# State-exchange attention with an MLP: state reads turned once through DRAM, scores of later batches kept in place, last rows in fewer transfers

## The chip, the cores and the metric

The kernel runs on one core of a Trainium2 chip. The metric is the device time in microseconds (us) of one execution; the median of several runs counts. One execution is also profiled, and the profile gives the start and the duration of each instruction on each engine: PE (matrix multiply; PEld is its weight load), ACT (activations and copies), DVE (elementwise work, reductions, 32x32 transposes), POOL, and SP, which here only issues DMAs. ACT issues DMAs too, on a queue of its own.

## The reference

For each of 8 batches and 8 heads there are 512 tokens `x` and 32 states, both of width 64. Tokens read from states, states read from tokens, and the two results, 544 rows per batch, go through one MLP of width 512 -> 2048 -> 512:

```
scores  = x @ state.T / 8        # 512 x 32
xread   = softmax(scores)  @ state
scores2 = state @ x.T / 8        # 32 x 512
sread   = softmax(scores2) @ x   # 32 x 64 per head
rows    = concat(xread, sread)   # heads side by side: (8 * 544) x 512
h       = rows @ w_in
g       = h if h >= 1, 0 if h <= -1, else (h + 1)**2 / 4
out     = g @ w_out
```

## The kernel before

Matmuls that need full precision are done as three matmuls of rounded pieces: each operand is split into a high part (names ending in `h`) and the rest (`l`), and high x high, high x rest and rest x high are added up in PSUM. So most lines of the matmul stream come in threes: L479, L480, L481 for the first MLP product (into the PSUM banks `h`), L537, L538, L539 for the second (into the accumulators `acc`).

The token rows of a batch never go through `w_in` as such. `xread` is attention times `state`, so the kernel multiplies `state` by `w_in` first (`sw_pair`, L426: eight column chunks per batch, two at a time, small matmuls of 64 rows x 32 columns of the array) and then the attention weights by that product (`g1`). `g2` is the product with `w_out`. A batch has 8 steps `(b, j)`, j = 0 to 7; step `(b, j)` issues `g1(b, j)` and then, in two parts, `g2` of the step before. Between them, the attention of the next batch b+1 is worked off:

- j = 0: `read2` (L358) of batch b, the matmuls of the state reads with the exponentials of `scores2`, already turned; `scale2`, which divides them by the sums on DVE; then the `sw` pieces 1 to 4 of batch b; then `scores` (L235) of batch b+1, 8 small products of 64 x 32 tiles into the PSUM tile with the tag `mm`, of which there is one; then `second`: the softmax over tokens, and `trade`.
- `trade` writes the exponentials `e2` to DRAM and reads them back in another order of partitions (one write and four reads, all on SP); a DVE transpose of 32x32 blocks (`turn_traded`, L336) at j = 2 completes the turn.
- j = 1: `keep2` turns the scaled state reads `rs` (128 x 128) by a PE transpose (L374, against `ident`) into another use of the tag `mm`, and `keep` copies the result on ACT (L379) into `srT`, which collects the state rows of all batches with features on the partitions.
- j = 2: `first`, the softmax over states. j = 4: the `sw` pieces 5 to 7 and piece 0 of the next batch, the last pair of them in the tag `mm`.

Batch 0 has an order of its own, written out by hand (`ORDER`, `Plan.emit`), which ends with step (0, 7); its `read2` and `keep2` are done together with those of batch 1 in steps (1, 0) and (1, 1). After it, order on each engine is set by a list scheduler: it takes instructions in program order, but an instruction whose inputs are ready may be put ahead of earlier ones while the engine would be idle by the scheduler's own reckoning. That order is fixed before the program runs; each engine then goes through its instructions strictly in turn.

After batch 7, "batch" 8 is the 256 state rows: `srT` is split by two DVE instructions (L808, L809), goes through `w_in` and `w_out` in 4 double steps, and the two blocks of 128 result rows are copied out of PSUM (L552 on ACT, L550 on DVE) and written by `store` (L559), 32 rows of one batch per transfer.

Of the kernel before, what the change touches and what calls it, by code (L numbers as in the profile page):

```python
# [8 lines left out]
F32 = mybir.dt.float32  # L9
# [4 lines left out]
ALU = mybir.AluOpType  # L14
# [94 lines left out]
def state_exchange_moe(  # L109
# [17 lines left out]
    nc = tc.nc  # L127
    B, P, NT, H, D = x.shape
    S = NT * P
    NS = 32  # L130
    DM = H * D
    NPR = H // 2
# [5 lines left out]
    TOK = S + NS  # L138
# [3 lines left out]
    small = ctx.enter_context(tc.tile_pool(name="small", bufs=1))  # L142
    const = ctx.enter_context(tc.tile_pool(name="const", bufs=1))
    work = ctx.enter_context(tc.tile_pool(name="work", bufs=2))
# [4 lines left out]
    dram = ctx.enter_context(tc.tile_pool(name="dram", bufs=2, space=bass.MemoryType.DRAM))  # L149

    def ps_acc(name):
        return ps.tile([P, DM], F32, tag="acc", bufs=4, name=name)
# [10 lines left out]
    def ps_mm(name):  # L163
        return ps.tile([P, 2, 512], F32, tag="mm", bufs=1, name=name)

    ident = small.tile([P, P], F32, name="ident")
# [14 lines left out]
    nc.gpsimd.memset(pad, 0.0)  # L181

    sb = const.tile([P, B, NPR, NS], F32, name="sb")
    srT = const.tile([P, NPR, B, NS], F32, name="srT")
    w32 = [const.tile([P, NPR, CI], F32, name=f"w32_{c}") for c in range(NC)]
    wo = {}
# [6 lines left out]
    def load_xt(b):  # L193
        xt = work.tile([P, 2, NPR, S // 2], F32, tag="xt", bufs=1, name=f"xt{b}")
        for i in range(2):
            nc.sync.dma_start(out=xt[:, i], in_=xt_in[b, i])
        return xt

    def load_xn(b):
        if b:  # L200
            xn = work.tile([P, NT, H, D], F32, tag="xn", bufs=1, name=f"xn{b}")
        else:
            xn = rawp.tile([P, NT, H, D], F32, tag="raw", name=f"xn{b}")
        nc.sync.dma_start(out=xn, in_=x[b])
        return xn

    class Attention:

# [8 lines left out]
        def scores(self, half=None):  # L217
            b = self.b
            if half != 1:
                if b:  # L220
                    sc = ps_mm(f"sc{b}")
                    self.sc = [sc[:, hh] for hh in range(2)]
                else:
                    self.sc = [ps_acc(f"sc{b}_{hh}") for hh in range(2)]
                self.z = work.tile([P, 2, S], F32, tag="z", bufs=1, name=f"z{b}")
                self.m1 = small.tile([P, 2 * NM], F32, tag="m1", name=f"m1_{b}")
                self.s1 = small.tile([P, 2 * NM], F32, tag="s1", name=f"s1_{b}")
            for pr in range(NPR):
                for hh in range(2):
                    rows = slice(hh * 64, hh * 64 + 64)  # L230
                    o = self.sc[hh][pr * NS:(pr + 1) * NS]
                    m = self.xt[rows, :, pr]
                    if half is not None:
                        o, m = o[:, half * S // 2:(half + 1) * S // 2], m[:, half]
                    nc.tensor.matmul(o, lhsT=sb[rows, b, pr], rhs=m, start=True, stop=True)  # L235

        def tokens(self, half):
            return slice(None) if half is None else slice(half * S // 2, (half + 1) * S // 2)
# [78 lines left out]
            )  # L317

        def trade(self):
            self.e2x = work.tile([P, NPR, 2 * P], F32, tag="tmp", name=f"e2x{self.b}")  # L320
            there = dram.tile([P, NT, 2 * P], F32, tag="e2d", name=f"e2d{self.b}")
            if self.b:
                nc.sync.dma_start(out=there, in_=self.e2.rearrange("p t q k -> p t (q k)"))
            else:
                for q in range(2):
                    nc.sync.dma_start(
                        out=there[:, :, q * P:(q + 1) * P], in_=self.e2[:, q].rearrange("p (t k) -> p t k", k=P)
                    )
            for t in range(NT):
                nc.sync.dma_start(  # L330
                    out=self.e2x[t * NS:(t + 1) * NS], in_=there[:, t].rearrange("(r n) k -> n r k", n=NS)
                )

        def turn_traded(self):
            e2 = self.e2.rearrange("p t q k -> p (t q k)" if self.b else "p q s -> p (q s)")
# [25 lines left out]
                        )  # L361

        def scale2(self):
            b = self.b
            self.rs = small.tile([P, 2, D], F32, tag="rs" if b else "rs_0", name=f"rs{b}")
            nc.vector.tensor_tensor(
                out=self.rs, in0=self.sr, in1=self.r2[:, :, None].broadcast_to([P, 2, D]), op=ALU.mult
            )

        def keep2(self):  # L370
            b = self.b
            self.turned2 = ps_mm(f"rt{b}") if b else atts[1].turned2
            self.rt = self.turned2[:, 0 if b else 1, :P]
            nc.tensor.transpose(  # L374
                out=self.rt, in_=self.rs.rearrange("p a d -> p (a d)"), identity=ident
            )

        def keep(self):
            nc.scalar.copy(  # L379
                out=srT[:, :, self.b], in_=self.rt.rearrange("p (g n) -> p g n", n=NS)  # L380
            )

        def second(self):
# [124 lines left out]
    def g1(b, j):  # L508
        hid = Hidden(b, j)
        for i in range(2):  # L510
            hid.product(i)
            hid.relu(i)
        hid.square()
        for i in range(2):
            hid.bound(i)
        hid.high()
        hid.low()
# [27 lines left out]
    def store(b, t):  # L545
        if t == 0:
            outs[b] = rawp.tile([P, NT, DM], F32, tag="raw", name=f"o{b}")
        o = outs[b][:, t]
        if b == B and t % 2:
            nc.vector.tensor_copy(o, acc[b][t])  # L550
        else:
            nc.scalar.copy(out=o, in_=acc[b][t])  # L552
        if b < B:
            r0 = b * TOK + t * P
            nc.scalar.dma_start(out=out[r0:r0 + P, :], in_=o)
        else:
            for i in range(4):
                r0 = (4 * t + i) * TOK + S
                (nc.sync if i % 2 else nc.scalar).dma_start(  # L559
                    out=out[r0:r0 + NS, :], in_=o[i * NS:(i + 1) * NS]  # L560
                )


# [51 lines left out]
    op = plan.op  # L615
# [25 lines left out]
    atts = {}  # L641
# [162 lines left out]
    for i, (b, j) in enumerate(steps):  # L804
        if (b, j) == (B, 0):
            sh, sl = (work.tile([P, NPR, B * NS], F32R, tag=t, name=f"s{t}") for t in ("ath", "atl"))
            src = srT.rearrange("p a b n -> p a (b n)")
            nc.vector.tensor_copy(sh, src)  # L808
            nc.vector.tensor_tensor(out=sl, in0=src, in1=sh.bitcast(F32), op=ALU.subtract)  # L809
            att_of[B] = (sh, sl)  # L810
        g1(b, j)
        if i + 1 < len(steps) and steps[i + 1][0] == B:
            for c in (2 * steps[i + 1][1], 2 * steps[i + 1][1] + 1):
                wi_split(c)
        before = steps[i - 1] if i else (0, NJ - 1)
        if b == B:
            g2(*before)
            continue
        nxt = atts[b + 1] = Attention(b + 1) if b + 1 < B and j == 0 else atts.get(b + 1)
        cut = 8 if j == 0 else 5  # L820
        g2(*before, (0, cut))
        if j == 0:
            if nxt:
                for k in (1, 0) if b == 1 else (b,):
                    atts[k].read2()
                for k in (1, 0) if b == 1 else (b,):
                    atts[k].scale2()
            halves = [
                sw_pair([(b, c), (b, c + 1)], [ps_acc(f"sw{b}_{c}_{hh}") for hh in range(2)]) for c in (1, 3)
            ]  # L830
            if nxt:
                nxt.scores()
                if b + 2 < B:
                    loaded["xt", b + 2] = load_xt(b + 2)
                loaded["xn", b + 1] = load_xn(b + 1)
            else:
                atts[b].read2()
            for split in halves:
                split()
            if nxt:  # L840
                nxt.second()
            else:
                atts[b].scale2()
        elif j == 1:
            for k in (1, 0) if b == 1 else (b,):
                atts[k].keep2()
            for k in (1, 0) if b == 1 else (b,):
                atts[k].keep()
        elif j == 2 and nxt:
            nxt.first()  # L850
        elif j == 4:
            last = [(b, 7)] + ([(b + 1, 0)] if nxt else [])
            own = ps_h(f"sw{b}_5")
            split = sw_pair([(b, 5), (b, 6)], own[1:])
            both = ps_mm(f"sw{b}_7")
            split2 = sw_pair(last, [both[:, hh] for hh in range(2)], both)
            split()
            split2()
            if nxt:
                nxt.halves()  # L860
        g2(*before, (cut, 8))
# [44 lines left out]
```

## Time and profile before

| | |
|---|---|
| time, median of 3 runs | 647.26 us (646.82 to 647.54) |
| the profiled execution's own time | 647.03 us |
| span of the profile | 645.3 us |
| PE busy | 635.3 us, 98% of the span |
| PE weight loads busy | 513.1 us, 80% |
| DVE busy | 347.0 us, 54% |
| ACT busy | 355.2 us, 55% |
| moved by DMA | 52.04 MB |

A time in the profile counts from the start of the span. A row of the timeline has the start, the duration, the engine, the line of the kernel, the operation, what it writes and reads, and in brackets how long its engine had been idle before it and what ended that. Rows that end in x2 or more join neighbours of one kind. Matmuls overlap: the distance between two starts tells what one costs, not its duration.

### The profile page before, as it was taken

How to read it: one execution, taken by the hardware profiler on the slowest of the kernel's cores; microseconds unless marked ns; L12 is line 12 of the kernel's file. 1: busy time of each engine (PE TensorE's matmuls, PEld its weight loads, DVE VectorE, ACT ScalarE, POOL GpSimd, SP SyncE). 2: the span in 40 equal slices, each digit the busy share in tenths (PEclk: the TensorE clock that was granted, in tenths of full speed). 3: DMA queues.
4: the chain of work that ended last, by engine and by line, in shares of the span. 5: the costliest groups of instructions: out<-in, count | busy, mean ns of one | idle time of the engine just before them, and what ended most of it. 6: DMA issues, size and time to landing. Idle time of an engine off the chain costs nothing.

```text
span 645.3 us, 10268 instructions
## 1 busy us (share of the span) xinstructions
PE 635.3 (98%) x4372; PEld 513.1 (80%) x4372; DVE 347.0 (54%) x492; ACT 355.2 (55%) x468; POOL 0.8 (0%) x7
## 2 busy tenths in 40 slices
PE   7899999999999999999999999999999999999997
PEld 6677777878787887878787887878787877788896
DVE  5999978642594338543574339433673344334431
ACT  4999865454565456444664457444654454444632
POOL 0000000000000000000000000000000000000000
PEclk9999999999999999999999999999999999999999
DMA  8996525000420006000520015000410010000101
GB/s 346 366 369 232 172 72 215 25 2 1 171 91 1 0 34 229 2 2 0 196 67 1 0 59 204 2 1 0 159 38 1 1 66 1 2 0 1 66 1 33
DMA packets 17757, 52.04 MB, mean 81 GB/s; under 512 B 1968, under 2 KB 7216, under 8 KB 14640
## 3 DMA queue, kind: packets, MB, share of 16 engines
q1 hardware_dynamic: 12768, 42.67, 17.9%
q10 hardware_dynamic: 4944, 8.72, 3.8%
q8 instruction: 34, 0.56, 0.4%
q14 instruction: 11, 0.09, 0.0%
HBM read 38.27 MB, written 13.11 MB: 80 GB/s over the span
## 4 chain that ended last, share of the span: by engine, by line
PE 95%; DVE 2%; ACT 1%; issue 0%; DMA 0%; ACTq 0%; POOL 0%; SPq 0%; POOLq 0%
PE acc L537 19%; PE acc L539 19%; PE acc L538 19%; PE h L479 10%; PE h L480 10%; PE h L481 10%; PE sw L426 4%; PE sc L235 1%; PE sr L358 1%; PE warmed L177 1%; DMA out_dram<-o 0%; ACT raw_o L591 0%; DVE z L274 0%; DVE sw_1l L442 0%; DVE m L253 0%
## 5 line engine op out<-in xcount | busy, mean ns | idle before, releaser
L537 PE MATMUL acc<-wo,gh 128*128 128x512 f32 x544 | 213.5, 392 | 0.0
L538 PE MATMUL acc<-wo,gh 128*128 128x512 f32 x544 | 211.9, 389 | 0.0
L539 PE MATMUL acc<-wo,gl 128*128 128x512 f32 x544 | 211.8, 389 | 0.0
L488 ACT ACTIVATE u<-h,half 128x512 f32<-128x512 f32 (+1 forms) x128 | 91.7, 716 | 179.3 <-PE h L481 170.4
L495 DVE SCALAR_TENSOR_TENSOR u<-u,h 128x512 f32<-128x512 f32 (+1 forms) x128 | 86.4, 714 | 184.2 <-ACT u L491 184.1
L537 PEld LDWEIGHTS acc<-wo,gh 128*128 128x128 f32 x544 | 102.1, 188 | 24.9 <-issue 3.7
L539 PEld LDWEIGHTS acc<-wo,gl 128*128 128x128 f32 x544 | 102.1, 188 | 21.6
L538 PEld LDWEIGHTS acc<-wo,gh 128*128 128x128 f32 x544 | 102.1, 188 | 20.6
L506 DVE TENSOR_TENSOR gl<-u,gh 128x1024 fp32r<-128x1024 f32 x68 | 83.3, 1224 | 55.3 <-ACT gh L501 55.3
L501 ACT CAST gh<-u 128x1024 fp32r<-128x1024 f32 x68 | 71.4, 1050 | 63.4 <-DVE u L495 63.4
L491 ACT ACTIVATE u<-u 128x1024 f32<-128x1024 f32 x68 | 72.2, 1061 | 1.8
L426 PE MATMUL sw<-w,sb 64*32 64x256 f32 x1024 | 32.3, 380 | 3.2 <-DVE w L599 2.2
L426 PEld LDWEIGHTS sw<-w,sb 64*32 64x32 f32 x1024 | 18.2, 106 | 12.8 <-DVE u L495 2.5
L552 ACT COPY o<-acc 128x512 f32<-128x512 f32 x33 | 19.0, 583 | 12.1 <-PE acc L539 12.1
L479 PE MATMUL h<-ath,sw_3h 128*128 128x512 f32 x64 | 25.1, 393 | 0.0
L479 PE MATMUL h<-ath,sw_5h 128*128 128x512 f32 x64 | 24.9, 390 | 0.0
L480 PE MATMUL h<-ath,sw_5l 128*128 128x512 f32 x64 | 24.9, 390 | 0.0
L481 PE MATMUL h<-atl,sw_3h 128*128 128x512 f32 x64 | 24.9, 389 | 0.0
L480 PE MATMUL h<-ath,sw_3l 128*128 128x512 f32 x64 | 24.9, 389 | 0.0
L481 PE MATMUL h<-atl,sw_5h 128*128 128x512 f32 x64 | 24.9, 389 | 0.0
L479 PE MATMUL h<-ath,sw_1h 128*128 128x512 f32 x60 | 24.4, 407 | 0.5 <-DVE u L495 0.4
L479 PE MATMUL h<-ath,sw_7h 128*128 128x512 f32 x60 | 23.5, 391 | 0.0
(160 smaller groups left out, 707.1 us busy)
## 6 DMA issues: line engine op xcount, KB each, us to landing
xt<-in_xt_dram SPq DMA_DIRECT2D x16, 512.0 KB, 5.4
raw_i<-in_moe_w_in_dram SPq DMA_DIRECT2D x8, 1024.0 KB, 7.1
raw_o<-in_moe_w_out_dram SPq DMA_DIRECT2D x8, 1024.0 KB, 11.6
xn<-in_x_dram SPq DMA_DIRECT2D x8, 1024.0 KB, 5.5
out_dram<-o ACTq DMA_DIRECT2D x32, 256.0 KB, 2.0
e2x<-e2d SPq DMA_DIRECT2D x32, 128.0 KB, 2.9
e2d<-e SPq DMA_DIRECT2D x7, 512.0 KB, 2.6
e2d<-e SPq DMA_DIRECT2D x2, 256.0 KB, 4.8
```

The source lines that it names most:

```text
L426: nc.tensor.matmul(banks[hh][pr * NS:(pr + 1) * NS, cols], lhsT=sb[rows, b, pr], rhs=w32[c][rows, pr], start=True, stop=True,)
L479: nc.tensor.matmul(o, lhsT=wh[:, k, sl], rhs=ah[:, k], start=first, stop=False)
L480: nc.tensor.matmul(o, lhsT=wl[:, k, sl], rhs=ah[:, k], start=False, stop=False)
L481: nc.tensor.matmul(o, lhsT=wh[:, k, sl], rhs=al[:, k], start=False, stop=last)
L488: nc.scalar.activation(out=u, in_=h, func=AF.Relu, scale=0.5, bias=half)
L491: nc.scalar.activation(out=self.u, in_=self.u, func=AF.Square)
L495: nc.vector.scalar_tensor_tensor(out=u, in0=u, scalar=1.0, in1=h, op0=ALU.min, op1=ALU.max)
L501: nc.scalar.copy(out=gh, in_=self.u)
L506: nc.vector.tensor_tensor(out=gl, in0=self.u, in1=gh.bitcast(F32), op=ALU.subtract)
L537: nc.tensor.matmul(a, lhsT=lh, rhs=oh, start=f == 0, stop=False)
L538: nc.tensor.matmul(a, lhsT=lh, rhs=ol, start=False, stop=False)
L539: nc.tensor.matmul(a, lhsT=ll, rhs=oh, start=False, stop=f == NF - 1)
```

## The change

Three edits.

First, the `scores` matmuls of batches 2 to 7 are tied to their place: each one gets an order edge (no wait for completion) behind the PE instruction written just before it, so the scheduler can't put it ahead of that one.

Second, the PE transposes and their ACT copies go (`keep2`, `keep`). `scale2` writes its result directly into `sread`, an SBUF tile that collects the scaled state reads of all batches. In step (7, 1) one trade through DRAM is issued for all of it, by the same function that e2 uses, and at (7, 6) in program order one DVE transpose writes `srT`. The function `trade` becomes free-standing, and for e2 it does what it did.

Third, the last rows of two batches are written by one transfer: each block of 128 rows takes two transfers of 64 rows, one from each of the two queues, in place of four of 32 rows, two from each.

```diff
+    sread = const.tile([P, NT, B, NS], F32, name="sread")
     srT = const.tile([P, NPR, B, NS], F32, name="srT")
...
+    def trade(a, name):
+
+        there = dram.tile([P, NT, 2 * P], F32, tag="there", name=f"{name}_there")
+        if a.shape[1] == NT:
+            nc.sync.dma_start(out=there, in_=a)
+        else:
+            for q in range(2):
+                nc.sync.dma_start(
+                    out=there[:, :, q * P:(q + 1) * P], in_=a[:, q].rearrange("p (t k) -> p t k", k=P)
+                )
+        traded = work.tile([P, NPR, 2 * P], F32, tag="tmp", name=f"{name}_x")
+        for t in range(NT):
+            nc.sync.dma_start(
+                out=traded[t * NS:(t + 1) * NS], in_=there[:, t].rearrange("(r n) k -> n r k", n=NS)
+            )
+        return traded
...
-                    nc.tensor.matmul(o, lhsT=sb[rows, b, pr], rhs=m, start=True, stop=True)
+                    made = nc.tensor.matmul(o, lhsT=sb[rows, b, pr], rhs=m, start=True, stop=True)
+                    if b > 1:
+                        tc.keep_in_program_order(made)
...
         def trade(self):
-            self.e2x = work.tile([P, NPR, 2 * P], F32, tag="tmp", name=f"e2x{self.b}")
...
+            self.e2x = trade(self.e2.rearrange("p t q k -> p t (q k)") if self.b else self.e2, f"e2_{self.b}")
...
         def scale2(self):
-            b = self.b
-            self.rs = small.tile([P, 2, D], F32, tag="rs" if b else "rs_0", name=f"rs{b}")
             nc.vector.tensor_tensor(
-                out=self.rs, in0=self.sr, in1=self.r2[:, :, None].broadcast_to([P, 2, D]), op=ALU.mult
-            )
-
-        def keep2(self):
-            b = self.b
-            self.turned2 = ps_mm(f"rt{b}") if b else atts[1].turned2
-            self.rt = self.turned2[:, 0 if b else 1, :P]
-            nc.tensor.transpose(
-                out=self.rt, in_=self.rs.rearrange("p a d -> p (a d)"), identity=ident
-            )
-
-        def keep(self):
-            nc.scalar.copy(
-                out=srT[:, :, self.b], in_=self.rt.rearrange("p (g n) -> p g n", n=NS)
+                out=sread.rearrange("p (q a) b d -> p q a b d", q=2)[:, :, :, self.b],
+                in0=self.sr.rearrange("p q (a d) -> p q a d", d=NS),
+                in1=self.r2[:, :, None, None].broadcast_to([P, 2, D // NS, NS]), op=ALU.mult,
             )
...
-            for i in range(4):
-                r0 = (4 * t + i) * TOK + S
+            rows = out.rearrange("(b r) d -> b r d", r=TOK)
+            for i in range(2):
+                b0 = 4 * t + 2 * i
                 (nc.sync if i % 2 else nc.scalar).dma_start(
-                    out=out[r0:r0 + NS, :], in_=o[i * NS:(i + 1) * NS]
+                    out=rows[b0:b0 + 2, S:], in_=o[i * 2 * NS:(i + 1) * 2 * NS]
                 )
...
         elif j == 1:
-            for k in (1, 0) if b == 1 else (b,):
-                atts[k].keep2()
-            for k in (1, 0) if b == 1 else (b,):
-                atts[k].keep()
+            if not nxt:
+                sreadx = trade(sread.rearrange("p t b n -> p t (b n)"), "sread")
         elif j == 2 and nxt:
             nxt.first()
+        elif j == 6 and not nxt:
+            nc.vector.transpose(
+                out=srT.rearrange("p r b n -> p (r b n)"), in_=sreadx.rearrange("p r k -> p (r k)")
+            )
```

More of the change, by code (lines that the diff above doesn't have):

```diff
@@ L319, in trade @@
         def trade(self):
-            self.e2x = work.tile([P, NPR, 2 * P], F32, tag="tmp", name=f"e2x{self.b}")
[L321 to L327, printed above, removed]
-                    )
-            for t in range(NT):
-                nc.sync.dma_start(
-                    out=self.e2x[t * NS:(t + 1) * NS], in_=there[:, t].rearrange("(r n) k -> n r k", n=NS)
-                )
+            self.e2x = trade(self.e2.rearrange("p t q k -> p t (q k)") if self.b else self.e2, f"e2_{self.b}")
         def turn_traded(self):
@@ L363, in scale2 @@
         def scale2(self):
-            b = self.b
-            self.rs = small.tile([P, 2, D], F32, tag="rs" if b else "rs_0", name=f"rs{b}")
             nc.vector.tensor_tensor(
-                out=self.rs, in0=self.sr, in1=self.r2[:, :, None].broadcast_to([P, 2, D]), op=ALU.mult
-            )
-        def keep2(self):
-            b = self.b
-            self.turned2 = ps_mm(f"rt{b}") if b else atts[1].turned2
-            self.rt = self.turned2[:, 0 if b else 1, :P]
-            nc.tensor.transpose(
-                out=self.rt, in_=self.rs.rearrange("p a d -> p (a d)"), identity=ident
-            )
-        def keep(self):
-            nc.scalar.copy(
-                out=srT[:, :, self.b], in_=self.rt.rearrange("p (g n) -> p g n", n=NS)
+                out=sread.rearrange("p (q a) b d -> p q a b d", q=2)[:, :, :, self.b],
+                in0=self.sr.rearrange("p q (a d) -> p q a d", d=NS),
+                in1=self.r2[:, :, None, None].broadcast_to([P, 2, D // NS, NS]), op=ALU.mult,
             )
```

## The prediction

> **What bounds the kernel now.** I read the page's busy times and its chain first, then the timeline of single engines at the three places that the change touches: the matmul stream around batch 2's scores, the stream around the eight transposes, and the last microseconds.
>
> ```profile
> span 645.3 us, 10268 instructions
> PE 635.3 (98%) x4372; PEld 513.1 (80%) x4372; DVE 347.0 (54%) x492; ACT 355.2 (55%) x468; POOL 0.8 (0%) x7
> PE 95%; DVE 2%; ACT 1%; issue 0%; DMA 0%; ACTq 0%; POOL 0%; SPq 0%; POOLq 0%
> ```
>
> PE is busy for 635.3 of 645.3 us and carries 95% of the chain that ended last. ACT and DVE are busy for a little over half the time. So an edit is worth what it takes out of the matmul stream, plus what it takes out of the stretch after the last matmul; work taken from ACT or DVE is worth nothing by itself, as long as no matmul was waiting for it.
>
> The first place is where two of batch 2's sixteen score matmuls (L235, two for each of the eight products) stand alone. Rows are start, duration, engine, line; in each group the matmul stream comes first, then weight loads and DVE.
>
> ```profile
> 87.99 0.39 PE L539 MATMUL acc<-wo,gl 128*128 128x512 f32 x1
> 88.31 1.04 PE L235 MATMUL sc<-xt,sb 64*32 64x512 f32 x2
> 89.28 0.50 PE L479 MATMUL h<-ath,sw_7h 128*128 128x512 f32 x1
> 89.62 0.39 PE L480 MATMUL h<-ath,sw_7l 128*128 128x512 f32 x1
> 99.61 1.96 PE L426 MATMUL sw<-w,sb 64*32 64x256 f32 x64
> 101.36 1.06 PE L235 MATMUL sc<-xt,sb 64*32 64x512 f32 x14
> 102.69 0.40 PE L480 MATMUL h<-ath,sw_1l 128*128 128x512 f32 x1
> 171.32 1.96 PE L426 MATMUL sw<-w,sb 64*32 64x256 f32 x64
> 173.07 1.06 PE L235 MATMUL sc<-xt,sb 64*32 64x512 f32 x16
> 174.40 0.40 PE L480 MATMUL h<-ath,sw_1l 128*128 128x512 f32 x1
> 89.28 0.19 PEld L479 LDWEIGHTS h<-ath,sw_7h 128*128 128x128 f32 x1 [0.84 <-DVE wo L610]
> 174.06 0.19 PEld L479 LDWEIGHTS h<-ath,sw_1h 128*128 128x128 f32 x1 [0.84 <-ACT sw_3h L440]
> 86.23 1.22 DVE L495 SCALAR_TENSOR_TENSOR u<-u,h 128x1024 f32<-128x1024 f32 x1
> 87.37 1.22 DVE L610 TENSOR_TENSOR wo<-wf,wo 128x1024 fp32r<-128x1024 f32 x1
> ```
>
> The second place is the transpose of the state reads (L374). The first row is the answer for its tile; the rest is the matmul stream around the pair of batches 0 and 1 and around the single one of batch 2.
>
> ```profile
> L374 PE MATMUL rt<-ident,rs x8: 270/270/293, 108.6 to 537.8; 128*128 128x128 f32 x8
> 107.70 0.39 PE L539 MATMUL acc<-wo,gl 128*128 128x512 f32 x1
> 108.38 0.39 PE L539 MATMUL acc<-wo,gl 128*128 128x512 f32 x1
> 109.08 0.39 PE L538 MATMUL acc<-wo,gh 128*128 128x512 f32 x1
> 180.09 0.39 PE L539 MATMUL acc<-wo,gl 128*128 128x512 f32 x1
> 180.66 0.39 PE L538 MATMUL acc<-wo,gh 128*128 128x512 f32 x1
> ```
>
> From 107.70 to 108.38 there are three matmuls, so the undisturbed pitch is 0.68 / 3 = 0.227 us. Every loss below is a start-to-start distance less the pitches that it would hold anyway; the 0.39 of a row is no cost, since the matmuls overlap.
>
> **Part 1, batch 2's scores.** L539 starts at 87.99 and the second matmul of the next product (L480) at 89.62: 1.63 us where two pitches, 0.45, would do. The lone pair of scores costs 1.18 us. Taking it back to its place costs nothing: from the start of the sw group to the L480 behind the scores it is 102.69 - 99.61 = 3.08 us with 14 score matmuls and 174.40 - 171.32 = 3.08 us with all 16. The matmuls of one product are hidden by the others, which run beside them in other parts of the array. For batches 3 to 7 the tie changes no order, the sixteen already follow sw there, as the row at 173.07 shows; I cost it at nothing.
>
> Would PE have been free to use that time? The product at 89.28 needs the h banks that the bound of step 7 (L495) reads, and that ends at 86.23 + 1.22 = 87.45, before 88.22, where the product would then start. The weight-load row names L610 as releaser, which ended at 87.37 + 1.22 = 88.59. If that were the true wait, 0.37 us would stay and the gain were 0.81. But behind the scores of batch 3 the same idle time of 0.84 stands with another releaser, so I read 0.84 as what going from small tiles back to the full array takes, with the name only the last semaphore seen in it; and L610 writes a weight tile that this product does not read. I take 1.18, with 0.81 as the other end.
>
> **Part 2, the transposes.** The pair costs 109.08 - 108.38 - 2 x 0.227 = 0.25 us, the single one 180.66 - 180.09 - 0.45 = 0.12. There are one pair and six singles (batches 2 to 7): 0.25 + 6 x 0.12 = 0.97 us, all in the matmul stream and all gone. The eight ACT copies behind them (L379) go too, worth nothing: no matmul waits for them, and ACT is 55% busy. The Trainium skill's page "TensorE: Matmul & The Clock Gate", Part 4, gives a transpose on PE as about 275 ns in a kernel's context; the tile's row agrees for the duration, 270 ns. By that figure the eight would be worth about 2.2 us (an estimate from that page), and the time 643.5. The distances above decide against it, because all but 0.12 us of each overlaps its neighbours.
>
> **Part 3, the trade that takes their place.** It is done once, in batch 7, by one write to DRAM and four reads on SP, and a single DVE transpose. The same trade exists for e2, and these rows price it; below them stand batch 7's rows for the place where it will run.
>
> ```profile
> 179.57 0.33 SPq L323 DMA_DIRECT2D e2d<-e  x1
> 182.23 1.75 SPq L330 DMA_DIRECT2D e2x<-e2d  x4
> e2x<-e2d SPq DMA_DIRECT2D x32, 128.0 KB, 2.9
> L336 DVE STREAM_TRANSPOSE e<-e2x 128x1024 f32<-128x1024 f32 x8 | 9.9, 1238 | 0.1
> 532.55 0.28 DVE L366 TENSOR_TENSOR rs<-sr,r 128x128 f32<-128x128 f32 x1
> 532.88 0.19 PEld L479 LDWEIGHTS h<-ath,sw_1h 128*128 128x128 f32 x1 [0.49 <-DVE rs L366]
> 536.39 1.28 DVE L495 SCALAR_TENSOR_TENSOR u<-u,h 128x512 f32<-128x512 f32 x2 [3.56 <-ACT u L491]
> 538.85 1.23 DVE L506 TENSOR_TENSOR gl<-u,gh 128x1024 fp32r<-128x1024 f32 x1 [1.17 <-ACT gh L501]
> 543.17 0.39 PE L539 MATMUL acc<-wo,gl 128*128 128x512 f32 x1
> 544.73 0.69 DVE L495 SCALAR_TENSOR_TENSOR u<-u,h 128x512 f32<-128x512 f32 x1 [2.80 <-ACT u L491]
> SPq L559 <- ACT o L552: 110.7, 1, 110.7
> ```
>
> The scaling ends at 532.83. The write takes 182.23 - 179.57 = 2.66 us until the first read can be issued, the fourth read starts 3/4 x 1.75 = 1.31 later and lands 2.9 after that: 539.7. SP has nothing else in that stretch: the last row is its wait of 110.7 us for the copy of the last output rows, which begins before 532, so nothing is queued behind the five DMAs that could come late. The transpose takes 1.24 us, as e2's does. I expect it on DVE behind L506, which ends at 540.08, so from 540.1 to 541.3, while the next bound comes at 544.73. What used to run there, the two casts of srT, moves behind the transpose and has some 50 us of matmuls of batch 7 as cover. Cost: 0.
>
> Both ends of this: nothing is waiting for the trade but the casts, so it can gain nothing. It loses if the DVE stream puts the transpose ahead of the bound at 536.39, where it would hold DVE until 540.9. Then gl would end 4.5 us later than 540.08, and its first user, L539 at 543.17, has 3.09 us of slack: 1.4 us lost. The scaling itself now writes runs of 32 numbers 1 KB apart instead of one block. Only in batch 7 does PE wait for it (the row at 532.88); nearest price 0.28 us for the whole instruction, so between -0.1 and +0.3, and I take 0: the count of elements is the same.
>
> **Part 4, the last rows.**
>
> ```profile
> 641.16 0.69 DVE L550 COPY o<-acc 128x512 f32<-128x512 f32 x1 [5.41 <-DMA out_dram<-o]
> 641.88 0.78 SPq L559 DMA_DIRECT2D out_dram<-o  x2
> 641.89 0.85 ACTq L559 DMA_DIRECT2D out_dram<-o  x2
> L559 ACTq DMA_DIRECT2D out_dram<-o x4: 374/406/445, 639.1 to 642.3; - x4
> out_dram<-o ACTq DMA_DIRECT2D x32, 256.0 KB, 2.0
> out_dram<-o ACTq DMA_DIRECT2D x4, 64.0 KB, 2.0
> ```
>
> After the copy both queues issue two transfers, one after the other; the last of them starts at 642.3 and the kernel ends when they have landed. With one each, the last starts at 641.89, about 0.41 earlier (half of 0.78 to 0.85). Twice the bytes in one transfer: 256 KB and 64 KB both land in 2.0 us from this queue, so 128 KB should too. Gain 0.41; bounds 0 (all bytes were under way together anyway) and 0.45, or -0.15 should the doubled transfer take longer. The Trainium skill's page "DMA: Bandwidth & Descriptors", section "Anatomy of one DMA", fits a DMA as about 2.0 us and the bytes over 436 GB/s, for the queue of another engine; by it (an estimate) 64 KB more take 0.15 us, the gain here would be 0.26 and the time 644.9. The two rows with 2.0 show no such slope.
>
> **Sum.** 1.18 + 0.97 + 0.41 = 2.56 us. The profiled execution took 647.03 us, its span of 645.3 and 1.73 around it: 644.47. The runs shown go from 646.82 to 647.54, and their median, 647.26, is 0.23 above the profiled one; carried to that median, the sum gives 644.70. I forecast 644.7.
>
> **Rivals.**
> 1. The gap at 88 us does not close: something else that is ready is put there, or PE waits. For it: the scheduler found PE idle at that point in its own reckoning, or it would not have moved the scores up. Against: the other small matmuls need banks that are taken (accumulators of batch 0, h banks). Gain 0.97 + 0.41 = 1.38, time 645.9.
> 2. The trade's transpose stands early in the DVE stream and holds the bound: 1.4 us lost, time 646.1. For it: the casts of srT at 540 were also moved up, so the transpose will be. Against: the eight e2 transposes had only 0.1 us of idle time ahead of them in all.
> 3. The tail gives nothing, since the same bytes have to land: time 645.1.
> 4. Slower: with the transposes gone, the PSUM tile "mm" is free from batch b+1's exponentials until its last sw pieces, and those, ready from the start, float up into the stream as batch 2's scores did. Each lone visit costs 1.18 us; three make the gain vanish (3.54 against 2.56), from four on it is slower by over 0.2%, and one in each of batches 1 to 7 gives 644.7 + 8.3 = 653.0. Against it: in the old kernel that tile was free too between the transpose's copy and the sw pieces, and with PE at 98% there is next to no idle time for something to float into.
>
> **How the numbers follow.** My forecast has 0.64, with rival 3 another 0.14 (still faster), rival 1 0.10, rival 2 0.07, rival 4 0.05. A change under 0.2%, 1.3 us, is about what a measurement of this kernel can't tell from none, so "faster" is below 645.97 and "slower" above 648.55. Faster: 0.64 + 0.14 + 0.07 of rival 1, whose time lies just inside that bound, = 0.85. Same: 0.03 of rival 1, 0.06 of rival 2 and 0.02 of rival 4 with two or three visits = 0.11. Slower: 0.03 of rival 4 and 0.01 of rival 2 with a late trade = 0.04. The range goes from 644.7 less 0.1 (scaling), less half the spread of the runs shown, 0.4, and less 0.4 for idle times around the changed places that may close with them, to 646.1, which takes in rivals 1 to 3: 643.8 to 646.1.
>
> **What would show it.** Right: one group of sixteen L235 matmuls in batch 2 and no L235 between 80 and 95 us; the product's first matmul 0.23 us behind the last L539; no matmul against the identity after the warm-up, and a pitch of 0.227 where they stood; one more DVE transpose of about 1.24 us in batch 7, with no matmul waiting behind it; one transfer per queue after the last copy; PE busy near 633.1 and about 3.8 us from last matmul to end. Wrong: small-tile matmuls in lone groups, a wait of DVE for the trade's DMA with PE idle 3 us behind it, or last transfers that land later than 2.0 us after issue.

## The result

The changed kernel is slower: 653.82 us against 647.04 us, medians of four runs each, a ratio of 1.0112 (95% interval 1.0091 to 1.0133). The forecast was 644.7, with a range to 646.1 and 0.04 for slower. The profiled execution took 653.65 us, with a span of 651.8, 6.5 more than before. Its page:

```profile
span 651.8 us, 10245 instructions
PE 632.8 (97%) x4364; PEld 512.7 (79%) x4364; DVE 348.1 (53%) x493; ACT 354.0 (54%) x460; POOL 0.8 (0%) x7
PE 95%; DVE 2%; ACT 1%; issue 0%; DMA 0%; ACTq 0%; POOL 0%; SPq 0%; POOLq 0%
```

PE is busy for 2.5 us less, in a longer span: the matmuls did gain, and the loss lies outside them. The matmul stream where the lone scores stood (start, duration, line):

```profile
88.02 0.39 PE L534 MATMUL acc<-wo,gl 128*128 128x512 f32 x1
88.24 0.39 PE L474 MATMUL h<-ath,sw_7h 128*128 128x512 f32 x1
88.47 0.39 PE L475 MATMUL h<-ath,sw_7l 128*128 128x512 f32 x1
```

The product follows the last L534 at the plain pitch. The chain of the kernel before, at three of the state reads (start, duration, line):

```profile
97.75 1.92 PE sr L358 x128
...
170.36 1.03 PE sr L358 x64
...
456.73 1.03 PE sr L358 x64
```

The same places in the chain of the changed kernel:

```profile
96.56 1.92 PE sr L366 x128
...
168.89 1.03 PE sr L366 x64
...
454.62 1.03 PE sr L366 x64
```

The lead is 1.19 us at the first (the scores), 1.47 at the second (0.28 for the pair of transposes) and 2.11 at the third (0.16 for each of four batches). By the last copy out of PSUM it is 2.49: it starts at 638.67 in place of 641.16. Then comes the end. Last matmul, copy and issues:

```profile
638.25 0.39 PE L534 MATMUL acc<-wo,gl 128*128 128x512 f32 x1
638.67 0.69 DVE L545 COPY o<-acc 128x512 f32<-128x512 f32 x1 [5.44 <-PE acc L534]
639.39 0.53 SPq L555 DMA_DIRECT2D out_dram<-o  x1
639.40 0.53 ACTq L555 DMA_DIRECT2D out_dram<-o  x1
```

and SP's wait at the end, with the DMA traffic from 636 us to the end in 40 slices:

```profile
SPq L900 <- DMA out_dram<-o: 10.9, 1, 10.9
```

```profile
GB/s 0 0 0 0 16 21 10 16 52 41 36 21 31 26 41 21 31 52 52 52 52 52 47 52 52 47 52 52 52 52 52 52 52 52 52 31 10 0 0 0
DMA packets 264, 0.52 MB, mean 33 GB/s; under 512 B 8, under 2 KB 8, under 8 KB 264
```

From the start of the last copy to the end of the span it is 651.8 - 638.67 = 13.1 us; before it was 645.3 - 641.16 = 4.1. That is 9.0 lost against 2.5 gained, and the difference, 6.5, is the whole change of the span. The last 0.52 MB move at no more than about 52 GB/s. In the kernel before, the same stretch:

```profile
GB/s 0 0 0 0 0 0 0 0 0 0 0 0 0 0 0 0 70 194 256 220 335 53 0 0 0 0 0 0 62 194 256 220 326 71 0 0 0 0 0 0
DMA packets 384, 0.52 MB, mean 56 GB/s; under 512 B 128, under 2 KB 128, under 8 KB 384
```

The packet counts are the clue. 256 packets of 2 KB carry the rows in both. The small ones beside them are 128 for 8 transfers before, 16 each, and 8 for 4 transfers after, 2 each. The Trainium skill's page "DMA: Bandwidth & Descriptors", section "Why a DMA increments its semaphore by 16 and not by 1", explains such a count: each DMA engine that takes part closes with one small write, and the number of engines is the largest one up to 16 that divides the outermost dimension of both sides. The new destination is two batches of 32 rows, so its outermost dimension is 2.

The traces hold a second count of the engines. The rows below are sums over a stretch: its bounds and length, the busy time of PE, PEld, DVE, ACT and POOL, PE's granted clock, and at the end the mean busy share of the core's 16 DMA engines and the GB/s that they moved. First a stretch of the kernel before, then one of the changed kernel:

```profile
643.00:643.50 0.50, 0.00 (x0) 0.00 (x0) 0.00 (x0) 0.00 (x0) 0.00 (x0) 1.00 0.95 258
```

```profile
643.00:649.00 6.00, 0.00 (x0) 0.00 (x0) 0.00 (x0) 0.00 (x0) 0.00 (x0) 0.50 0.13 51
```

A share of 0.95 is 15 of 16 engines at work; 0.13 is two.

### The profile page after: what moved, and what is told of

The parts are those of the page before. It is cut to its first block, busy times and chain, and to the rows that moved or that the text cites. A ratio compares the mean times of both kernels' runs of the same rounds, so it can differ in the third digit from the quotient of the medians.

```text
span 651.8 us, 10245 instructions
## 1 busy us (share of the span) xinstructions
PE 632.8 (97%) x4364; PEld 512.7 (79%) x4364; DVE 348.1 (53%) x493; ACT 354.0 (54%) x460; POOL 0.8 (0%) x7
## 4 chain that ended last, share of the span: by engine, by line
PE 95%; DVE 2%; ACT 1%; issue 0%; POOL 0%; POOLq 0%
PE acc L532 19%; PE acc L533 19%; PE acc L534 19%; PE h L474 10%; PE h L475 10%; PE h L476 10%; PE sw L421 4%; PE sr L366 1%; PE sc L253 1%; PE warmed L177 1%; ACT raw_o L587 0%; DVE z L294 0%; DVE m L273 0%; DVE zt L301 0%; DVE u L490 0%
## 5 line engine op out<-in xcount | busy, mean ns | idle before, releaser
L534 PE MATMUL acc<-wo,gl 128*128 128x512 f32 x544 | 211.7, 389 | 0.0
L534 PEld LDWEIGHTS acc<-wo,gl 128*128 128x128 f32 x544 | 102.1, 188 | 21.4
L421 PE MATMUL sw<-w,sb 64*32 64x256 f32 x1024 | 32.3, 380 | 3.2 <-DVE w L595 2.2
L421 PEld LDWEIGHTS sw<-w,sb 64*32 64x32 f32 x1024 | 18.2, 106 | 12.8 <-DVE u L490 2.5
L475 PE MATMUL h<-ath,sw_1l 128*128 128x512 f32 x60 | 23.4, 391 | 0.0
```

Source lines behind the costliest of these rows:

```text
L421: nc.tensor.matmul(banks[hh][pr * NS:(pr + 1) * NS, cols], lhsT=sb[rows, b, pr], rhs=w32[c][rows, pr], start=True, stop=True,)
L475: nc.tensor.matmul(o, lhsT=wl[:, k, sl], rhs=ah[:, k], start=False, stop=False)
L534: nc.tensor.matmul(a, lhsT=ll, rhs=oh, start=False, stop=f == NF - 1)
```

## The experiments

Theory T: that dimension sets the number of DMA engines, and the new transfers run on 2 of 16. Theory S: a destination in separate pieces is slow by itself. Theory R: the trade or the tie delays the end, and the transfers are only where it is seen. "Tail" below is the time from the start of the last copy to the end of the span.

### The parts one by one

The changed kernel with the old last rows (e1):

```diff
-            rows = out.rearrange("(b r) d -> b r d", r=TOK)
-            for i in range(2):
...
+            for i in range(4):
+                r0 = (4 * t + i) * TOK + S
+                (nc.sync if i % 2 else nc.scalar).dma_start(
+                    out=out[r0:r0 + NS, :], in_=o[i * NS:(i + 1) * NS]
+                )
```

> The changed kernel with the last rows written as before: four transfers of 32 rows per block. Theory T (the loss is in the last transfers: one whose DRAM side has 2 as its outermost dimension runs on 2 DMA engines instead of 16) and theory S (the loss is in the last transfers, because a destination in separate pieces is slow by itself): from the start of the last copy to the end 4.1 us as before (13.1 in the changed kernel), and the 2.48 us that the matmul stream gained stay: 647.04 - 2.48 = 644.6. Theory R (the trade or the tie delays the end, the transfers are only where it is seen): above 650.

Measured: 644.89 us, ratio 0.9968 (0.9956 to 0.9980). Its last copy and page:

```profile
640.28 0.69 DVE L545 COPY o<-acc 128x512 f32<-128x512 f32 x1 [5.43 <-PE acc L534]
```

```profile
span 644.3 us, 10249 instructions
```

The tail is 4.0 us. So the loss is in the last transfers, and theory R is refuted.

The kernel before with only the new last rows (e2), the same edit the other way round.

> The kernel before with only the last rows changed to transfers of two batches. T and S: the whole loss of the tail, 13.13 - 4.14 = 9.0 us, without any gain: 656.0. R: 647.0.

Measured: 656.10, ratio 1.0136 (1.0119 to 1.0153), tail 654.7 - 641.61 = 13.1. The edit alone costs 9 us.

The kernel before with only the tie (e3):

```diff
+                    if b > 1:
+                        tc.keep_in_program_order(made)
```

> The kernel before with only the scores of batches 2 to 7 tied to their place. Prediction's part 1: 1.18 us less, 645.9. If the place is filled by another instruction or PE waits there: 647.0, or 646.2 if the wait named in the profile was the true one.

Measured: 645.91 against 647.08, 1.17 less; ratio 0.9982 (0.9972 to 0.9992). That is the 1.18 of part 1. The other end, 0.81, isn't excluded by the interval (0.5 to 1.8 us), but by the rows above: the lead at the first state reads is 1.19.

The kernel before with only the trade in place of the transposes (e4; old tail, no tie).

> The kernel before with only the eight PE transposes replaced by the one trade through DRAM and one DVE transpose. Prediction's part 2: 0.97 us less, 646.1. From the changed kernel's stream, which gains 0.28 for the pair and 0.16 in each of batches 2 to 7: 1.2 to 1.3 less, 645.8. If the trade were in the way of the end (R): above 650.

Measured: 645.54, 1.54 less; ratio 0.9978 (0.9967 to 0.9989), or 0.7 to 2.1 us. This holds both 0.97 and 1.24; the chain rows above decide for the larger.

### How many engines

One transfer of four batches per block (e5): outermost dimension 4.

```diff
-            for i in range(2):
-                b0 = 4 * t + 2 * i
...
+            (nc.sync if t % 2 else nc.scalar).dma_start(out=rows[4 * t:4 * t + 4, S:], in_=o)
```

> The changed kernel with one transfer of four batches (128 rows, outermost dimension 4 on the DRAM side) per block, block 0 from ACT's queue and block 1 from SP's. Theory T (as many DMA engines as the outermost dimension allows): 4 engines for all 512 KB; two engines moved about 50 GB/s in the changed kernel, so four move 100, block 1's 256 KB take 2.6 us in place of some 1.2 and the end comes 1 to 2 us later than with four transfers of 32 rows: 645.5 to 647. Theory S (pieces are slow by themselves): four pieces, not better than the changed kernel's 653.8.

Measured: 648.93, ratio 1.0019 (1.0005 to 1.0032); tail 646.1 - 637.89 = 8.2. The traffic from 636 us on:

```profile
GB/s 0 0 0 0 49 41 8 24 0 8 49 57 73 65 105 105 97 97 114 97 105 89 73 65 81 89 73 97 97 97 81 65 32 24 16 0 0 0 0 0
DMA packets 264, 0.52 MB, mean 52 GB/s; under 512 B 8, under 2 KB 8, under 8 KB 264
```

There are 8 small packets for 2 transfers, 4 each, and about twice the rate. From 639 to 644 us the share of busy DMA engines is 0.25, which is 4 of 16:

```profile
639.00:644.00 5.00, 0.00 (x0) 0.00 (x0) 0.00 (x0) 0.00 (x0) 0.00 (x0) 0.87 0.25 88
```

More pieces in one transfer, and yet faster: that speaks against S. But T's number, 645.5 to 647, was too low. It took the full rate from the first byte, and the first transfer began slowly, at 0 to 57 GB/s for 2 us.

The state rows of a block ordered by state first, batch second, so that 64 rows go out as 16 x 4 (e6). The casts read `srT` in that order:

```diff
-            src = srT.rearrange("p a b n -> p a (b n)")
+            src = srT.rearrange("p a (t i) n -> p (a t) n i", i=4)
...
-            rows = out.rearrange("(b r) d -> b r d", r=TOK)
+            rows = out.rearrange("(b r) d -> r b d", r=TOK)
             for i in range(2):
-                b0 = 4 * t + 2 * i
+                r0 = S + i * NS // 2
                 (nc.sync if i % 2 else nc.scalar).dma_start(
-                    out=rows[b0:b0 + 2, S:], in_=o[i * 2 * NS:(i + 1) * 2 * NS]
+                    out=rows[r0:r0 + NS // 2, 4 * t:4 * t + 4], in_=o[i * 2 * NS:(i + 1) * 2 * NS]
                 )
```

> The changed kernel with the state rows of a block ordered by state first and batch second (the two casts of srT read it in that order), and two transfers per block of 64 rows each, whose DRAM side has 16 rows outermost and 4 batches inside: 64 separate pieces of 2 KB, one transfer on each queue. T: 16 engines, the tail as before or shorter by one issue time, 0.41 (the prediction's part 4): 644.2 to 644.6 against 644.6 worked out for four transfers. S: more pieces than in the changed kernel, at least 653.8.

Measured: 645.17, ratio 0.9959 (0.9945 to 0.9974); tail 643.4 - 638.88 = 4.5. From 636 us on, and the issues:

```profile
GB/s 0 0 0 0 0 0 0 0 0 0 0 188 244 343 288 255 100 0 0 0 0 0 0 0 0 0 188 255 332 277 266 100 0 0 0 0 0 0 0 0
DMA packets 320, 0.52 MB, mean 71 GB/s; under 512 B 64, under 2 KB 64, under 8 KB 320
out_dram<-o ACTq DMA_DIRECT2D x2, 128.0 KB, 2.7
```

```profile
L555 ACTq DMA_DIRECT2D out_dram<-o x2: 567/610/654, 636.8 to 639.6; - x2
```

There are 16 small packets per transfer, and the rate is that of the kernel before (343 GB/s at most, 335 there), with every 2 KB row apart from its neighbour in the transfer: S is refuted. The time lies 0.6 us above T's forecast; the kernel before took 647.55 in this series, 0.5 more than in the first. But the tail isn't shorter than with four transfers, 4.0. The issue takes 0.57 to 0.65 us, not 0.41, and the landing 2.7 us, not 2.0. So part 4's gain of 0.41 isn't there on 16 engines either.

The same order, one transfer of 128 rows (32 x 4) per block (e7).

```diff
+            (nc.sync if t % 2 else nc.scalar).dma_start(out=rows[S:, 4 * t:4 * t + 4], in_=o)
```

> The same order of rows, and one transfer per block: 32 rows outermost, 4 batches inside, 128 pieces, block 0 from ACT's queue and block 1 from SP's. T: 16 engines, 644.2 to 644.8 (256 KB in one transfer landed in 2.0 us elsewhere). S: at least 653.8.

Measured: 644.88, ratio 0.9959 (0.9944 to 0.9973); tail 643.4 - 639.22 = 4.2. Its counts:

```profile
DMA packets 288, 0.52 MB, mean 71 GB/s; under 512 B 32, under 2 KB 32, under 8 KB 288
```

The two transfers have 16 small packets each. One transfer does what four did, and no more.

Two-batch transfers for block 0 alone, four transfers for block 1 (e8).

> The changed kernel with two-batch transfers for block 0 only, and four transfers of 32 rows for block 1, the last. T: block 0's 256 KB go through two engines at 50 GB/s, 5.2 us from about 637.2 to 642.4; the share of block 1 on those two engines, 32 KB, comes behind or between and takes 0.65 us more; end about 1.5 to 2 us later than with four transfers for both: 646 to 646.7. If only the last transfers count: 644.6.

Measured: 649.06, ratio 1.0021 (1.0008 to 1.0033); tail 646.8 - 638.18 = 8.6. Its counts:

```profile
DMA packets 324, 0.52 MB, mean 49 GB/s; under 512 B 68, under 2 KB 68, under 8 KB 324
```

68 is 2 x 2 + 4 x 16. Only two transfers, of the block that is issued 2.8 us earlier (636.07 against 638.90), run on two engines, and it is still slower than the kernel before. The last block's four transfers, on 16 engines, land late, after a median of 5.3 and 6.6 us in place of 1.7 and 2.0, and from 642 to 645 us only two engines' worth of work is left:

```profile
out_dram<-o SPq DMA_DIRECT2D x2, 64.0 KB, 5.3
out_dram<-o ACTq DMA_DIRECT2D x2, 64.0 KB, 6.6
```

```profile
642.00:645.00 3.00, 0.00 (x0) 0.00 (x0) 0.00 (x0) 0.00 (x0) 0.00 (x0) 0.69 0.13 48
```

This fits T's account that the last block's share on those two engines waits behind the first block. Again the size was missed, by 2.4 us; the traffic began slowly here too.

Last, the dimension alone, inside one batch: each of the eight transfers of 32 rows written as 2 x 16 rows, the even ones first (e9), or as 16 x 2 (e10, the same line with q=16). The casts of `srT` read the rows in the matching order.

```diff
-                    out=out[r0:r0 + NS, :], in_=o[i * NS:(i + 1) * NS]
+                    out=out[r0:r0 + NS, :].rearrange("(n q) d -> q n d", q=2), in_=o[i * NS:(i + 1) * NS]
```

> Four transfers of 32 rows per block, each inside one batch, but written as 2 x 16 rows: first the even rows, then the odd ones (the casts of srT read the rows in that order, so that the output is the same). Theory T (the outermost dimension of the DRAM side sets the number of DMA engines): two engines for all eight transfers, the tail as long as in the changed kernel, 13 us in place of 4, about 653.5, and 2 small packets per transfer in the DMA counts. Theory S (one transfer over two batches is slow, because its pieces lie far apart): each transfer stays in one batch, 644.6.

> The same as the last one, with the 32 rows written as 16 x 2: outermost dimension 16. T: 16 engines, 644.6 to 645.0, tail 4.0 to 4.6, 16 small packets per transfer. S and any theory by which the interleaved order itself is slow: the same as the last one.

Measured, e9: 652.85, ratio 1.0086 (1.0068 to 1.0105). Last copy, then page, then DMA from 636 us on:

```profile
639.13 0.69 DVE L545 COPY o<-acc 128x512 f32<-128x512 f32 x1 [5.42 <-PE acc L534]
```

```profile
span 651.5 us, 10249 instructions
```

```profile
GB/s 0 0 0 0 0 0 32 11 42 42 42 37 26 21 42 21 37 48 48 53 53 53 53 48 48 53 53 53 53 48 48 53 53 53 48 48 37 0 0 0
DMA packets 272, 0.52 MB, mean 34 GB/s; under 512 B 16, under 2 KB 16, under 8 KB 272
```

e10: 645.37, ratio 0.9973 (0.9964 to 0.9983), tail 643.6 - 639.10 = 4.5:

```profile
DMA packets 384, 0.52 MB, mean 69 GB/s; under 512 B 128, under 2 KB 128, under 8 KB 384
```

Same number of transfers, same 64 KB each, one batch each, rows of 2 KB in both: with 2 outermost the tail is 12.4 us and each transfer has 2 small packets, with 16 it is 4.5 us and 16. From 643 to 649 us the share of busy DMA engines in e9 is 0.13, as in the changed kernel. That settles T against S, for the outermost dimensions that were tried: 2, 4, 16 and 32. The time of e10 is 0.4 us above the forecast 645.0; its transfers took 0.55 to 0.86 us each to issue.

### A shorter end

The last copy shared by columns between DVE and ACT, with the old last rows (e11):

```diff
-            nc.vector.tensor_copy(o, acc[b][t])
+            nc.vector.tensor_copy(o[:, :DM // 2], acc[b][t][:, :DM // 2])
+            nc.scalar.copy(out=o[:, DM // 2:], in_=acc[b][t][:, DM // 2:])
```

> The changed kernel with four transfers of 32 rows, and the last copy out of PSUM split by columns between DVE and ACT, 256 each in place of 512 on DVE (0.69 us): about 0.3 us less than with four transfers alone, 644.3, since the last transfers wait for the copy and everything behind it shifts. If ACT starts later than DVE or the shorter copy is not half as long: 644.6.

Measured: 644.68, ratio 0.9965 (0.9952 to 0.9977), not told apart from e1. The timelines of DVE and ACT:

```profile
639.34 0.42 DVE L545 COPY o<-acc 128x256 f32<-128x256 f32 x1 [5.41 <-PE acc L534]
```

```profile
639.79 0.37 ACT L546 COPY o<-acc 128x256 f32<-128x256 f32 x1 [2.59 <-DVE o L545]
```

ACT waited for DVE's half: 0.82 us in sum in place of 0.69. Both halves read one accumulator tile and write one output tile; which of the two makes ACT wait is not shown. The fastest versions are those with part 1 and part 2 and all 16 engines in the last transfers: e1, e6, e7, e10 and e11, with ratios of 0.996 to 0.997. Their intervals overlap, so none of them is the best. With part 1 or part 2 alone, e3 and e4 have 0.998.

## Why the prediction was wrong

**Part 1** held: 1.18 us forecast, 1.19 in the chain, 1.17 in the time of e3. The reading that the named releaser (L610) was not what the product waited for held too: the product starts 0.22 us behind the last matmul.

**Part 2** held, and was sized too low: 0.97 forecast, 0.28 + 6 x 0.16 = 1.24 by the chain. The distances were taken over two pitches only. In the kernel before, the matmuls behind a transpose went on at a slightly longer pitch. Behind the one of batch 2, there are nine pitches between these rows:

```profile
180.66 0.39 PE L538 MATMUL acc<-wo,gh 128*128 128x512 f32 x1
182.75 0.39 PE L480 MATMUL h<-ath,sw_1l 128*128 128x512 f32 x1
```

They take 2.09 us in place of 9 x 0.227 = 2.04. These 0.05 us went too, and with the 0.12 of the forecast they make up the 0.16.

**Part 3** held. The trade's rows in the changed kernel, first SP, then DVE:

```profile
530.50 0.34 SPq L212 DMA_DIRECT2D sread_there<-sread  x1
533.20 1.73 SPq L220 DMA_DIRECT2D sread_x<-sread_there  x4
```

```profile
536.49 1.23 DVE L501 TENSOR_TENSOR gl<-u,gh 128x1024 fp32r<-128x1024 f32 x1 [1.17 <-ACT gh L496]
538.34 1.25 DVE L846 STREAM_TRANSPOSE srT<-sread_x 128x1024 f32<-128x1024 f32 x1 [0.63 <-DMA sread_x<-sread_there]
542.21 1.28 DVE L490 SCALAR_TENSOR_TENSOR u<-u,h 128x512 f32<-128x512 f32 x2 [2.62 <-ACT u L486]
```

The transpose stands behind the `gl` of that step, as expected, waits 0.63 us for the trade and is done 2.6 us before the next bound. The wait was not in the working, which had the trade landed at 539.7, ahead of the end of `gl` at 540.08. It landed at 538.34, in a stream that runs 2.4 us ahead at that place (536.49 against 538.85 at `gl`), so about 1.0 us later than worked out; the slack took it up. Rival 2 did not occur.

**Part 4** is the step that failed: "Twice the bytes in one transfer: 256 KB and 64 KB both land in 2.0 us from this queue, so 128 KB should too." It ordered transfers by bytes. The two rows had 128 and 32 as the outermost dimension of the destination; the new transfer has 2, and no transfer of the kernel before was near to that in shape. So it ran on 2 DMA engines in place of 16. The worst end of this term, -0.15, had no row behind it either. The prediction took the fit of bytes from the Trainium skill's page "DMA: Bandwidth & Descriptors"; the rule on engines in a later section of that page, cited above, spoke against the change. As a change of the time, the term measured +9.0 us in place of -0.41: from the start of the last matmul to the end it is 651.8 - 638.25 = 13.6 us, where the prediction had 3.8. With it, the rest comes out: 647.04 - 2.49 + 9.0 = 653.6, against 653.82. Also with 16 engines the tail is 0.2 (e7) to 0.5 us (e6) longer than e1's, so a saved issue was worth nothing here: the longer form takes longer to issue and to land.

**The rivals.** Rival 3 had the right place and stopped at no gain. Rival 4 gave 653.0, near to the measured time only by luck. Its mechanism did not occur: in the chain of the changed kernel the sw matmuls (L421) of each batch from 1 to 6 still stand in two groups of 64, one behind the state reads and one in step j = 4, and there are no lone ones. Rival 1 is refuted by the rows at 88 us.

**What stays open.** Transfers on two or four engines start slowly: in the changed kernel 10 to 52 GB/s, 28 on average, in the first 5 us of traffic, then 47 to 52 until they run out. The forecasts for e5 and e8 left this out and came out too low. No run shows what causes it.

## What to carry to other kernels

Before transfers are joined, look at the outermost dimension of both sides as the instruction carries it: joining two runs of 32 rows turned 32 into 2, and 16 DMA engines into 2. With the joined rows reordered so that 16 or 32 came outermost, all 16 engines worked again, but the joined transfers were no faster than their parts (tails of 4.2 and 4.5 us against 4.0). And a row that prices a transfer must be near in shape, not only in bytes; the small packets in a stretch of DMA counts, divided by the transfers in it, tell how many engines each one used.

## What the hardware showed

- Two DMA engines together moved 51 GB/s once the rate was steady (changed kernel and e9, 643 to 649 us), and four moved 88 on average from 639 to 644 us and 114 at most (e5). That is some 25 GB/s for one engine. The Trainium skill's page "DMA: Bandwidth & Descriptors", section "Specifications", gives about 27 GiB/s, which is 29 GB/s; the runs stay a little below that.
- A transfer with three dimensions took 0.53 to 0.86 us to issue (the changed kernel, e6, e7, e10), where the last ones of the kernel before, with two dimensions, took 0.31 to 0.45. With 2 or 4 outermost, the first one on ACT's queue took longer still: 1.37 us in the changed kernel, 1.15 in e5 and 1.50 in e9, but 0.65 to 0.68 in e6, e7 and e10, with 16 or 32 outermost. Why is not shown.

```profile
L555 ACTq DMA_DIRECT2D out_dram<-o x2: 527/947/1367, 636.6 to 639.4; - x2
```
